# Attention, gated mixing and a gated projection on one core: the last product by seven block products, and smaller moves with it

## The chip, the cores and the metric

The kernel runs on one core of one Trainium2 chip. The metric is the device time of the program in microseconds; the kernel before takes 701.81 us, the median of three runs (699.28 to 704.09). All numbers in this document are float32 or float32r ("fp32r", the form of float32 that TensorE multiplies).

## The reference, cut to what matters

Three stages follow one another, for 4 batches of 576 tokens:

```python
# 1 attention: 8 heads of 64, causal, with a bias from a running sum of s
x = attention(q, k, v, s)                      # (4, 576, 512)
# 2 mixing with the previous token, then two gated products
k = np.maximum(xk @ w_k, 0.0)                  # 512 -> 1024
v = k * k @ w_v                                # 1024 -> 512
r = 1.0 / (1.0 + np.exp(-(xr @ w_r)))          # 512 -> 512
x = r * v
# 3 spatial gating
h = gelu_tanh(x @ w_in)                        # 512 -> 1024
u, v = (h[..., :d_ff // 2], h[..., d_ff // 2:])
v_n = (v - mu) / np.sqrt(var + 1e-06) * g_ln
v_s = np.einsum('ts,bsd->btd', w_sg, v_n) + b_sg[None, :, None]
gated = u * v_s
return (x + gated @ w_out).astype(np.float32)  # 512 -> 512
```

## The kernel before

Every float32 product is made of three fp32r products: each operand is split into a high half (the value cast to fp32r) and a low half (the value less its high half), and high times high, low times high and high times low are summed in one PSUM bank (a PSUM bank holds the sum of a chain of matmuls). The cast is a copy, mostly on ScalarE (ACT, helper `copy`, L71), the low half a subtraction on VectorE (DVE, helper `minus`, L74).

A scheduler orders each engine's instructions by a model of their times, within priorities that the code sets. Attention (generator `attend`) and the second stage (generator `moe1`) run interleaved until about 370 us; `moe1` goes over eight units of half a batch (288 tokens) and ends at about 506 us. In each unit `r` is made from a tanh: `rt = 0.5 * tanh(..) + 0.5` for a whole unit on DVE (L657), and then each of four tiles of `k*k @ w_v` is multiplied by it (L663) and stored to DRAM (`x2_d`). The weights come as 64-bit words; `convert` turns them into two halves.

The third stage goes batch by batch, from the loop at L975. Its functions, in the order of their matmuls for a batch b:

- `v_side(b)`: five row tiles of `v`, 56 matmuls, gelu on ACT, row statistics on DVE;
- `project(b-1)`: the last product of the batch before, `w_out` times gated, as eight tiles `po` of 128 x 288, 12 matmuls each (`mm3`, L690); DVE adds the residual `xf` (L943) and SyncE's queue stores each tile;
- `u_side(b)`: eight tiles `pu`, 12 matmuls each, gelu on ACT into `ut`;
- `norm(b)`: on DVE and ACT, beside the two above; the root by ACT's Sqrt, a reciprocal and one Newton step on DVE;
- `x_load(b+1)`: the next batch from DRAM and its halves;
- `gate(b)`: eight tiles `pg`, 14 matmuls each; for each tile DVE scales it (L930) and multiplies it by `ut` (L931) into `gf`, ACT casts the high half `gh`, DVE makes the low half `gl`.

All these tiles share six PSUM banks (`ps_b`): a matmul chain can start when the reader of the tile six places earlier is done. After the last batch `project` follows `gate` at once; elsewhere other matmuls lie between them.

Of the kernel before, what the change touches and what calls it, by code (L numbers as in the profile page):

```python
# [8 lines left out]
F32 = mybir.dt.float32  # L9
# [36 lines left out]
ENG = {"ia": "P", "mx": "D", "ca": "D", "p0": "P", "cl": "D", "qh": "D", "ql": "D", "kh": "A", "kl": "D", "vh": "A", "vl": "D", "xh": "A", "xl": "D", "fh": "A", "fl": "D", "rs": "D", "bh": "A", "bl": "D", "nh": "D", "nl": "D", "gh": "A", "gl": "D"}  # L46
# [6 lines left out]
def block_kernel(ctx: ExitStack, tc: tile.TileContext, qkv, vb, s, w_r, w_k, w_v, mu, w_in, w_out, w_sgT, g_ln, b_sg, out):  # L53
# [51 lines left out]
    def convert(w, c, n, t):  # L105
# [11 lines left out]
        nc.vector.scalar_tensor_tensor(ti, lw, 29, ti, ALU.logical_shift_right, ALU.bitwise_or)  # L117
        half = pool.tile([P, 2, 512], F32R, tag=name, name=name)
        copy("A" if att is not None else "D", half[:, 0], t)
        minus(ENG["cl"], half[:, 1], t, half[:, 0])  # L120
# [475 lines left out]
    def moe1():  # L596
# [29 lines left out]
        for u in range(2 * B):  # L626
# [30 lines left out]
            (nc.gpsimd if ENG["rs"] == "P" else nc.vector).tensor_scalar(rt, rt, 0.5, 0.5, ALU.mult, ALU.add)  # L657
            tc.cur_priority -= PM
            for m in range(4):
# [3 lines left out]
                nc.vector.tensor_tensor(rt[:, m], pm[:, 0:HD], rt[:, m], ALU.mult)  # L663
# [136 lines left out]
    def x_load(b):  # L800
        pool = pb if b % 2 else w2
        xf = pool.tile([P, 4, S], F32, tag="xf", name="xf")
        for hf in range(2):
            nc.sync.dma_start(xf[:, :, hf * HD : (hf + 1) * HD], x2_d[b][hf])
# [4 lines left out]
        xs[b] = xf, xh, xl, x4  # L809
        yield  # L810
        for c in range(4):
            copy(ENG["bh"], xh[:, c], xf[:, c])
            minus(ENG["bl"], xl[:, c], xf[:, c], xh[:, c])
            yield
        copy("D", x4[:, :, 0:D], xf[:, :, 4 * P :])
        minus("D", x4[:, :, D:], xf[:, :, 4 * P :], x4[:, :, 0:D])
# [3 lines left out]
    for size in moe1():  # L820
# [17 lines left out]
        if att is None and w2 is None:  # L838
# [5 lines left out]
            temps = w2.tile([P, 5, 512], F32, tag="vt", name="cvt")  # L844
            lws = conversions([(wi, c, n) for n in (1, 0) for c in range(4)], lambda i: temps[:, i % 5])
# [6 lines left out]
    def v_side(b, xh, xl, x4):  # L852
        vt = w2.tile([P, 5, DM], F32, tag="vt", name="vt")
        mv = mvs[b % 2]
        for t in range(5):
# [3 lines left out]
            if t < 4:  # L859
# [4 lines left out]
                nc.scalar.activation(vt[:, t], pv, AF.Gelu_apprx_tanh)  # L864
            else:
# [5 lines left out]
                vs = vt[:m, t]  # L871
# [4 lines left out]
            nc.vector.bn_stats(st[:m], vt[:m, t])  # L876
# [3 lines left out]
    def u_side(b, xh, xl):  # L880
        ut = pb.tile([P, 4, S], F32, tag="ut", name="ut")
        for m in range(4):
            for hf in range(2):
                hs = slice(hf * HD, (hf + 1) * HD)
                pu = ps_b.tile([P, 512], F32, tag="b", name="pu")
                mm3(pu[:, 0:HD], wi, m * P, xh[:, :, hs], xl[:, :, hs])
                nc.scalar.activation(ut[:, m, hs], pu[:, 0:HD], AF.Gelu_apprx_tanh)
        return ut

    def norm(b, vt, mv):  # L890
# [6 lines left out]
        nc.vector.tensor_tensor(t1, rs, rs, ALU.mult)  # L897
        nc.vector.tensor_tensor(t1, t1, var, ALU.mult)
        nc.vector.tensor_scalar(t1, t1, -0.5, 1.5, ALU.mult, ALU.add)
        nc.vector.tensor_tensor(rs, rs, t1, ALU.mult)  # L900
        vh, vl = ([xtp.tile([P, DM], F32R, tag=f"xt{t}", name=n) for t in range(4)] for n in ("vh", "vl"))
        v4 = const.tile([P, DM], F32R, tag="mask", name="v4")
        for t in range(5):
            m = P if t < 4 else D
            vs = vt[:m, t]
# [8 lines left out]

    def gate(b, ut, vh, vl, v4):
        gh = pb.tile([P, 4, S], F32R, tag="gh", name="gh")
        gl = pb.tile([P, 4, S], F32R, tag="gl", name="gl")
        for d in range(4):
            ds = slice(d * P, (d + 1) * P)
            for hf in range(2):  # L920
                hs = slice(hf * HD, (hf + 1) * HD)
                pg = ps_b.tile([P, 512], F32, tag="b", name="pg")
                for c in range(4):
                    nc.tensor.matmul(pg[:, 0:HD], vh[c][:, ds], wg[0][c][:, hs], start=(c == 0), stop=False)  # L924
                    nc.tensor.matmul(pg[:, 0:HD], vh[c][:, ds], wg[1][c][:, hs], start=False, stop=False)  # L925
                    nc.tensor.matmul(pg[:, 0:HD], vl[c][:, ds], wg[0][c][:, hs], start=False, stop=False)  # L926
# [4 lines left out]
                nc.vector.tensor_tensor(gf, gf, ut[:, d, hs], ALU.mult)  # L931
                copy(ENG["gh"], gh[:, d, hs], gf)
                minus(ENG["gl"], gl[:, d, hs], gf, gh[:, d, hs])
        return gh, gl

    def project(b, xf, gh, gl):
        for hf in range(2):
            hs = slice(hf * HD, (hf + 1) * HD)
            for m in range(4):
                po = ps_b.tile([P, 512], F32, tag="b", name="po")  # L940
                mm3(po[:, 0:HD], wo, m * P, gh[:, :, hs], gl[:, :, hs])
                ot = pb.tile([P, HD], F32, tag="ot", name="ot", bufs=3)
                nc.vector.tensor_tensor(ot, po[:, 0:HD], xf[:, m, hs], ALU.add)  # L943
                nc.sync.dma_start(out[b, m * P : (m + 1) * P, hs], ot)
# [4 lines left out]
    wg = [[], []]  # L949
    for c, tags in enumerate(SLOTS):  # L950
        if len(tags) == 2:
            halves = [w1p.tile([P, S], F32R, tag=t, name=f"wg{c}") for t in tags]
        else:
            place = xtp.tile([P, 2, S], F32R, tag=tags[0], name=f"wg{c}")
            halves = [place[:, 0], place[:, 1]]
# [90 lines left out]
```

## Time and profile before

| | |
|---|---|
| median of three runs | 701.81 us (699.28 to 704.09) |
| profiled execution | 701.87 us, of which the span from the first to the last instruction 700.0 us |
| TensorE (PE) busy | 666.8 us, 95% of the span, 4638 matmuls |
| VectorE (DVE) busy | 535.2 us, 76% |
| ScalarE (ACT) busy | 425.0 us, 61% |
| GpSimd (POOL) busy | 33.1 us, 5% |
| mean granted TensorE clock | 0.992 |

The profile is one execution. Busy time is the time in which an engine has an instruction under way; matmuls are pipelined, so the duration of one matmul is longer than the distance to the next, and what a matmul costs is read from the length of a whole chain. An idle stretch of an engine is put down to what released it.

### The profile page before, as it was taken

To read this page: it belongs to the slowest core of one execution; us is meant where nothing else is said; L and a number is where in the kernel's file an instruction comes from. 1 tells how busy PE (TensorE), PEld (TensorE's weight loads), DVE (VectorE), ACT (ScalarE), POOL (GpSimd) and SP (SyncE) were. 2 spreads that over 40 slices of the span, in tenths; PEclk is the share of its full clock that TensorE was granted. 3 is DMA by queue.
4 is the path that set the end of the run, shared out by engine and by line. 5 is a ranking of instruction groups with operands and counts; after the bars stand their busy time and mean duration, and the time that the engine had idled before them with its cause. 6 is when DMAs were issued, how large, how long until landed. Compare 5 with 4: busy or idle time off the path is not lost.

```text
span 700.0 us, 12906 instructions
## 1 busy us (share of the span) xinstructions
PE 666.8 (95%) x4638; PEld 620.8 (89%) x4638; DVE 535.2 (76%) x1341; ACT 425.0 (61%) x1011; POOL 33.1 (5%) x86
## 2 busy tenths in 40 slices
PE   7799888999998999999999999999999999999998
PEld 4578866988888989988999999999998998998997
DVE  8999899898989899899887796743847564564543
ACT  5789797778868986896895745725523233133120
POOL 6122100000000000000000000000000000000000
PEclk9999999999999999999999999999999999999999
DMA  8894442352443333423202700004240300300101
GB/s 267 238 286 152 148 137 63 92 154 80 126 118 101 90 109 93 133 81 108 85 22 79 272 10 35 1 18 163 67 112 18 119 1 15 122 2 9 60 1 68
DMA packets 39831, 67.47 MB, mean 96 GB/s; under 512 B 6908, under 2 KB 23400, under 8 KB 39736
## 3 DMA queue, kind: packets, MB, share of 16 engines
q1 hardware_dynamic: 39768, 66.66, 31.2%
q8 instruction: 36, 0.59, 0.4%
q14 instruction: 27, 0.22, 0.1%
HBM read 51.85 MB, written 10.19 MB: 89 GB/s over the span
## 4 chain that ended last, share of the span: by engine, by line
PE 64%; DVE 19%; ACT 6%; DMA 4%; issue 3%; SPq 2%; DVEq 0%; POOL 0%; ACTq 0%
PE m L677 25%; PE po L690 7%; PE pu L690 7%; DVE pr L374 3%; PE pg L925 2%; PE pg L926 2%; PE pg L924 2%; DMA rb<-rd 2%; DVE qk L74 2%; PE pv L863 2%; PE pv L862 2%; PE pv L861 2%; PE av L527 2%; DVE ptl L546 2%; ACT pr L400 2%
## 5 line engine op out<-in xcount | busy, mean ns | idle before, releaser
L400 ACT ACTIVATE pr<-pr,nm 128x448 f32<-128x448 f32 (+4 forms) x144 | 85.1, 592 | 21.2 <-DVE nm L374 20.6
L677 PE MATMUL m<-xh,wk 128*128 128x288 f32 x512 | 83.2, 301 | 0.0
L677 PE MATMUL m<-kh,wv 128*128 128x288 f32 x512 | 79.1, 297 | 0.0
L677 PEld LDWEIGHTS m<-xh,wk 128*128 128x128 f32 x512 | 73.1, 191 | 1.8 <-ACT xh L71 0.7
L677 PEld LDWEIGHTS m<-kh,wv 128*128 128x128 f32 x512 | 71.5, 188 | 0.4
L374 DVE CUSTOM_DVE_ANT_0 pr<-s,mask 128x448 f32<-128x448 f32 (+4 forms) x144 | 64.9, 453 | 8.3 <-PE s L360 6.5
L359 PE MATMUL s<-qk 128*128 128x288 f32 (+4 forms) x144 | 46.8, 327 | 8.6 <-DVE nh L374 5.9
L71 ACT CAST xh<-xf 128x288 fp32r<-128x288 f32 (+1 forms) x80 | 36.1, 480 | 22.7 <-DVE xf L616 10.7
L677 PE MATMUL m<-xl,wk 128*128 128x288 f32 x256 | 47.4, 301 | 0.0
L545 ACT CAST pth<-t 128x512 fp32r<-128x512 f32 (+1 forms) x72 | 38.2, 532 | 13.4 <-PE t L542 12.3
L360 PE MATMUL s<-qk 128*128 128x288 f32 (+4 forms) x144 | 44.1, 309 | 1.8 <-DVE kl L74 1.8
L546 DVE TENSOR_TENSOR ptl<-t,pth 128x512 fp32r<-128x512 f32 (+1 forms) x72 | 43.9, 614 | 2.2 <-ACT pth L545 1.9
L677 PE MATMUL m<-kl,wv 128*128 128x288 f32 x256 | 44.2, 299 | 0.0
L638 ACT ACTIVATE kf<-m 128x288 f32<-128x288 f32 x64 | 26.2, 411 | 28.7 <-PE m L677 28.2
L74 DVE TENSOR_TENSOR xl<-xf,xh 128x288 fp32r<-128x288 f32 (+1 forms) x80 | 39.0, 508 | 5.7 <-PE m L677 4.2
L71 ACT CAST gh<-gf 128x288 fp32r<-128x288 f32 x32 | 13.9, 433 | 45.8 <-DVE gf L931 45.8
L542 PE MATMUL t<-ident,pr 128*128 128x128 f32 x252 | 40.0, 277 | 1.6 <-DVE ptl L546 1.0
L677 PE MATMUL m<-xh,wr 128*128 128x288 f32 x256 | 40.8, 298 | 0.5 <-ACT kf L638 0.3
L610 ACT ACTIVATE xf<-xt,mu 128x288 f32<-128x288 f32 x64 | 33.4, 535 | 12.2 <-DVE xl L74 8.3
L690 PE MATMUL pu<-xh,wi 128*128 128x288 f32 x256 | 39.9, 295 | 0.0
L690 PE MATMUL po<-gh,wk 128*128 128x288 f32 x256 | 39.3, 296 | 0.0
L359 PEld LDWEIGHTS s<-qk 128*128 128x128 f32 x144 | 27.3, 190 | 12.9 <-DVE nh L374 8.1
(299 smaller groups left out, 1738.9 us busy)
## 6 DMA issues: line engine op xcount, KB each, us to landing
kld<-qkv SPq DMA_DIRECT2D x28, 288.0 KB
qld<-qkv SPq DMA_DIRECT2D x24, 288.0 KB
x_d<-rt SPq DMA_DIRECT2D x8, 576.0 KB
xf<-x_d SPq DMA_DIRECT2D x8, 576.0 KB
outT<-ot SPq DMA_DIRECT2D x32, 144.0 KB
vld<-qkv SPq DMA_DIRECT2D x24, 160.0 KB
qk<-qk SPq DMA_DIRECT2D x24, 144.0 KB
rb<-rd SPq DMA_DIRECT2D x24, 128.0 KB
```

The costliest lines, as they stand in the source:

```text
L71: nc.scalar.copy(dst, src) if eng == "A" else nc.vector.tensor_copy(dst, src)
L74: (nc.gpsimd if pick(engines) == "P" else nc.vector).tensor_tensor(dst, a, b.bitcast(F32), ALU.subtract)
L359: nc.tensor.matmul(dst, qk[0][:, 0, qs], qk[0][:, 1, ks], start=True, stop=False)
L360: issued[0] = nc.tensor.matmul(dst, qk[1][:, 0, qs], qk[1][:, 1, ks], start=False, stop=True)
L374: nc.vector.tensor_tensor_reduce(out=dst, in0=src, in1=msk, scale=-0.125, scalar=first, op0=ALU.add, op1=ALU.min, accum_out=acc)
L400: i = nc.scalar.activation(dst, dst, AF.Exp, bias=nm[:, col : col + 1], scale=-1.0, accum_out=w.sm[:, col : col + 1])
L542: issued[0] = nc.tensor.transpose(bank[:, o : o + P], x, ident)
L545: nc.scalar.copy(pth[:, cols], bank[:, 0:o])
L546: nc.vector.tensor_tensor(ptl[:, cols], bank[:, 0:o], pth[:, cols].bitcast(F32), ALU.subtract)
L610: nc.scalar.mul(xf, xp, mu1[:, j, c : c + 1])
L677: i = nc.tensor.matmul(dst, w(x, c, m), xx[:, c], start=(n + c == 0), stop=(n == 2 and c == w.nk - 1))
L690: nc.tensor.matmul(dst, w(x, c, m), xx[:, c], start=(n + c == 0), stop=(n == 2 and c == w.nk - 1))
```

## The change

The last product becomes one with seven block products where there were eight (Strassen's, in Winograd's form): `w_out` and gated are cut in two by two blocks, sums and differences of blocks of `w_out` are made once (`quarters`: three blocks as they are, four sums), those of gated once a batch in `gate` (tile `tf`, halves kept in `tp`), and `project` makes, for each of two row halves, seven products of six matmuls and joins them with sums `u`. For this:

- `project` has 84 matmuls a batch where it had 96. DVE adds six sums `u` a batch; the residual is read again from DRAM into `ot` and GpSimd adds `u` to it (`emit`; in the last batch it lies in `xr`, and half of these adds are DVE's); DVE adds the PSUM tile, as before. One product of each half is copied out of PSUM by ACT.
- `gate` goes through the second half of its tiles in another order (right half first), and each batch has eight subtractions and eight pairs of halves for `tf` more, two pairs fewer for `gh` and `gl`.
- `w_out` is no longer converted to halves by `conversions`, but assembled, summed and split in `quarters`, which comes after the first batch's `gate`. `project` of the first batch moves behind `u_side(1)`.
- `norm`'s root is three Newton steps from an integer start, all on DVE; ACT needs no Sqrt, and the program holds 2 loads of ACT's function tables where it held 11. `vh` is cast by ACT where DVE did it.
- `x_load` fetches half a batch at a time into one buffer, and the tiles `vt` and `ut` are two pieces each.
- `rt`'s scaling at L657 is gone: the factor 0.5 goes into `wv`'s halves, and the product takes `rt + 1` in the same instruction.

The diff, cut to its core:

```diff
+        if w is wv:
+            nc.scalar.mul(half[:, 0], t, 0.5)
+            nc.vector.scalar_tensor_tensor(half[:, 1], t, 0.5, half[:, 0].bitcast(F32), ALU.mult, ALU.subtract)
...
-            (nc.gpsimd if ENG["rs"] == "P" else nc.vector).tensor_scalar(rt, rt, 0.5, 0.5, ALU.mult, ALU.add)
...
-                nc.vector.tensor_tensor(rt[:, m], pm[:, 0:HD], rt[:, m], ALU.mult)
+                nc.vector.scalar_tensor_tensor(rt[:, m], rt[:, m], 1.0, pm[:, 0:HD], ALU.add, ALU.mult)
...
-        nc.scalar.activation(rs, var, AF.Sqrt)
-        nc.vector.reciprocal(rs, rs)
+        nc.vector.tensor_scalar(rs.bitcast(I32), var.bitcast(I32), 1, 0x7FFFFFFF, ALU.logical_shift_right, ALU.bitwise_xor)
+        nc.vector.tensor_scalar(rs, rs, 0.33885 * 2.0**-64, None, ALU.mult)
         t1 = const.tile([P, 5], F32, tag="t1", name="t1")
...
+        for _ in range(3):
+            nc.vector.tensor_tensor(t1, rs, rs, ALU.mult)
+            nc.vector.scalar_tensor_tensor(t1, t1, -0.5, var, ALU.mult, ALU.mult)
+            nc.vector.scalar_tensor_tensor(rs, t1, 1.5, rs, ALU.add, ALU.mult)
...
+    def halves(k, c, x):
+
+        copy("A", tp[k][0][c], x)
+        minus("D", tp[k][1][c], x, tp[k][0][c])
...
+                if d < 2 and hf:
+                    nc.vector.tensor_tensor(tf[:, 0, c], gf, ut[d // 2][:, d % 2, hs], ALU.mult)
+                    less(tf[:, 1, c], tf[:, 0, c], last)
+                    halves(1, c, tf[:, 1, c])
+                    continue
+                nc.vector.tensor_tensor(gf, gf, ut[d // 2][:, d % 2, hs], ALU.mult)
+                if d >= 2:
+                    if hf:
+                        less(tf[:, 1, c], gf, tf[:, 1, c])
+                        less(tf[:, 0, c], gf, tf[:, 0, c])
+                    else:
+                        less(tf[:, 1, c], gf, tf[:, 1, c])
                 copy(ENG["gh"], gh[:, d, hs], gf)
                 minus(ENG["gl"], gl[:, d, hs], gf, gh[:, d, hs])
+                if d >= 2:
+                    for k, x in ((2, 1), (3, 0)) if hf else ((4, 1),):
+                        halves(k, c, tf[:, x, c])
...
+            for y, z in ((0, 0), (1, 0), (0, 1)):
+                for c in range(2):
+                    nc.tensor.matmul(dst, wq[a][:, y, c, ms], x[z][c], start=(n == 0), stop=(n == 5))
...
+            if last:
+                ot = xr[:, i, hs]
+            else:
+                pool, n = ((pb, 3), (w2, 2))[outs[0] % 5 // 3]
+                outs[0] += 1
+                ot = pool.tile([P, HD], F32, tag="ot", name="ot", bufs=n)
+                nc.sync.dma_start(ot, x2_d[b][hf][:, i])
+            (nc.vector if last and m else nc.gpsimd).tensor_tensor(ot, ot, u, ALU.add)
+            add(ot, ot, bank)
+            nc.sync.dma_start(out[b, i * P : (i + 1) * P, hs], ot)
+
+        for m in range(2):
+            ms = slice(m * P, (m + 1) * P)
+            u1, u2 = place(0), place(1)
+            nc.scalar.copy(u1, part("11", block(0, 0)))
+            add(u2, u1, part("s2", tp[2]))
+            emit(m, 0, u1, part("12", block(1, 0)))
+            u3 = place(2)
+            add(u3, u2, part("s3", tp[3]))
+            p5 = part("s1", tp[1])
+            emit(2 + m, 1, u3, p5)
+            add(u2, u2, p5)
+            emit(m, 1, u2, part("s4", block(1, 1)))
+            emit(2 + m, 0, u3, part("22", tp[4]))
```

The scheduler orders the new instructions. The three places below show what it made of them where it matters for the argument. Names: `po` and `p`, `ps` are PSUM tiles of the projection (after the change one each block product, in the order 11, s2, 12, s3, s1, s4, 22 of the code); numbers behind a name tell tiles apart.

DVE after the last tile of the last batch's `gate`, before the change: it finishes the tile and then only adds the residual.

```order
L930 SCALAR_TENSOR_TENSOR gf<-pg,g_sb,b_sb 128x288
L74 TENSOR_TENSOR gl<-gf,gh 128x288
L931 TENSOR_TENSOR gf<-gf,ut 128x288
L74 TENSOR_TENSOR gl<-gf,gh 128x288
L943 TENSOR_TENSOR ot<-po,xf 128x288 x8
```

Behind the last tile's two products stand one subtraction and the eight adds.

The same place on DVE after the change, from the last tile's first instruction to the add that frees tile `p_8627` (product 12).

```order
L957 SCALAR_TENSOR_TENSOR gf<-pg,g_sb,b_sb 128x288
L74 TENSOR_TENSOR gl<-gf,gh 128x288
L74 TENSOR_TENSOR wg_6314<-tf,tp 128x288
L74 TENSOR_TENSOR wg_6294<-tf,wg_6304 128x288
L963 TENSOR_TENSOR gf<-gf,ut_7682 128x288
L937 TENSOR_TENSOR tf<-gf,tf 128x288
L993 TENSOR_TENSOR us<-ps_8619,us 128x288
L74 TENSOR_TENSOR gl<-gf,gh 128x288
L993 TENSOR_TENSOR us<-ps_8637,us 128x288
L74 TENSOR_TENSOR tp<-tf,tp 128x288
L1014 TENSOR_TENSOR xr<-xr,us 128x288
L993 TENSOR_TENSOR xr<-ps_8645,xr 128x288
```

Two more rows, `us<-ps_8645,us` and `xr<-p_8627,xr`, follow there. Where three instructions stood between the last gate tile and the adds, a mix of gate work and sums stands now.

DVE at the end of the program after the change, behind the sums of product s3 of the second half.

```order
L1014 TENSOR_TENSOR xr<-xr,us 128x288
L993 TENSOR_TENSOR xr<-ps_8710,xr 128x288
L993 TENSOR_TENSOR us<-ps_8710,us 128x288
L993 TENSOR_TENSOR xr<-p_8731,xr 128x288
L1014 TENSOR_TENSOR xr<-xr,us 128x288
L993 TENSOR_TENSOR xr<-ps_8721,xr 128x288
```

Behind the add of the last product (`p_8731`) two more adds stand now; before, the add of the last tile was DVE's last instruction.

PE at the start of the last projection, before the change: tile after tile, all from `gh` and `gl`.

```order
L927 MATMUL pg<-wg_6338,v_8223 128x288
L928 MATMUL pg<-wg_6338,v_8223 128x288
L690 MATMUL po<-gh,wk_6601 128x288
L690 MATMUL po<-gh,wk_6609 128x288
L690 MATMUL po<-gh,wk_6617 128x288
```

Nothing of the gate but `gh` and `gl` is needed for this.

The same place on PE after the change: single matmuls of products s2, 12 and s3 are started early, and 12 is finished only after s3 and s4.

```order
L988 MATMUL p_8611<-gh,w_6829 128x288 x4
L988 MATMUL p_8611<-gl,w_6829 128x288 x2
L988 MATMUL ps_8619<-tp,ws_6851 128x288
L988 MATMUL p_8627<-gh,w_6832 128x288
L988 MATMUL ps_8637<-wg_6305,ws_6844 128x288
L988 MATMUL ps_8645<-gh,ws_6839 128x288 x4
L988 MATMUL ps_8645<-gl,ws_6839 128x288 x2
L988 MATMUL ps_8656<-gh,ws_6848 128x288 x4
L988 MATMUL ps_8656<-gl,ws_6848 128x288
L988 MATMUL ps_8619<-tp,ws_6851 128x288 x3
```

Products that need the last tile's sums have moved behind those that need only earlier ones.

DVE beside the projection of the second and the third batch, which the norm of the next batch shares; before the change, from the second residual add on.

```order
L943 TENSOR_TENSOR ot<-po,xf 128x288
L892 TENSOR_SCALAR var<-mv_6296 128x5
L895 RECIPROCAL rs<-rs 128x5
L897 TENSOR_TENSOR t_8210<-rs 128x5
L898 TENSOR_TENSOR t_8210<-t_8210,var 128x5
L943 TENSOR_TENSOR ot<-po,xf 128x288
L899 TENSOR_SCALAR t_8210<-t_8210 128x5
L900 TENSOR_TENSOR rs<-rs,t_8210 128x5
L906 TENSOR_SCALAR vt<-vt,mv_6296,rs 128x512 x4
```

Three adds are through before the wide steps of the norm begin.

The same stretch after the change.

```order
L993 TENSOR_TENSOR u<-ps_7560,u 128x288
L907 TENSOR_SCALAR var<-mv_6290 128x5
L909 TENSOR_SCALAR rs<-var 128x5
L910 TENSOR_SCALAR rs<-rs 128x5
L913 TENSOR_TENSOR t_7800<-rs 128x5
L914 SCALAR_TENSOR_TENSOR t_7800<-t_7800,var 128x5
L993 TENSOR_TENSOR ot<-ps_7568,ot 128x288
L993 TENSOR_TENSOR u<-ps_7568,u 128x288
L915 SCALAR_TENSOR_TENSOR rs<-t_7800,rs 128x5
L993 TENSOR_TENSOR ot<-p_7593,ot 128x288
```

Sums `u` stand between the residual adds, and the wide steps of the norm (L906, now L921) come later against them.

## Rows read from the trace of the kernel before

**Rows 1.** Windows by stage: start:end, us, busy us (count) of each engine, clock, DMA.

```profile
100.00:150.00 50.00, 45.91 (x316) 41.56 (x316) 46.81 (x126) 37.88 (x96) 2.34 (x7) 0.97 0.35 101
...
350.00:500.00 150.00, 149.38 (x1081) 145.61 (x1082) 106.98 (x239) 88.50 (x192) 0.71 (x3) 1.00 0.22 75
500.00:696.70 196.70, 196.69 (x1357) 188.46 (x1355) 108.11 (x252) 53.91 (x106) 0.00 (x0) 1.00 0.15 48
```

**Rows 2.** Waits of PE from 125 to 350 us: total us, times, longest.

```profile
PE s L359 <- DVE nh L374: 5.9, 8, 1.7
PE av L527 <- DVE ptl L546: 2.7, 4, 1.6
```

**Rows 3.** Chain of waits that ended last, from 530 us: start, us, what.

```profile
537.04 12.79 PE po L690 x96
...
683.89 12.81 PE po L690 x96
696.73 0.46 DVE ot L943
```

**Rows 4.** Groups by line, 480 to 700 us: shapes, count, busy us, mean ns, idle before.

```profile
L930 DVE SCALAR_TENSOR_TENSOR gf<-pg,g_sb,b_sb 128x288 f32<-128x288 f32 x32 | 16.5, 515 | 27.0 <-PE pg L928 26.8
L74 DVE TENSOR_TENSOR gl<-gf,gh 128x288 fp32r<-128x288 f32 x32 | 14.4, 451 | 3.8 <-ACT gh L71 3.6
L943 DVE TENSOR_TENSOR ot<-po,xf 128x288 f32<-128x288 f32 x32 | 14.2, 452 | 9.8 <-PE po L690 9.6
...
L887 ACT ACT_TABLE_LOAD x4 | 5.1, 1283 | 31.3 <-PE pu L690 31.3
```

**Rows 5.** Timeline of DVE in the last gate: first instruction of its last two tiles.

```profile
682.07 0.52 DVE L930 SCALAR_TENSOR_TENSOR gf<-pg,g_sb,b_sb 128x288 f32<-128x288 f32 x1 [0.60 <-PE pg L928]
...
683.92 0.52 DVE L930 SCALAR_TENSOR_TENSOR gf<-pg,g_sb,b_sb 128x288 f32<-128x288 f32 x1 [0.61 <-PE pg L928]
```

**Rows 6.** Timeline of DVE beside the second projection (590 to 605 us).

```profile
595.75 2.36 DVE L906 TENSOR_SCALAR vt<-vt,mv,rs 128x512 f32<-128x512 f32 x5
...
604.03 0.82 DVE L943 TENSOR_TENSOR ot<-po,xf 128x288 f32<-128x288 f32 x2
```

**Rows 7.** Timeline of POOL, 0 to 88 us: its widest arithmetic.

```profile
15.13 1.40 POOL L454 TENSOR_SCALAR pr<-pr,rc 128x128 f32<-128x128 f32 x1 [1.97 <-DVE rc L412]
...
43.98 0.85 POOL L454 TENSOR_SCALAR pr<-pr,rc 128x128 f32<-128x128 f32 x1 [0.63 <-PE t L438]
...
54.97 1.88 POOL L74 TENSOR_TENSOR qk<-qld,qk 64x256 fp32r<-64x256 f32 x2 [7.98 <-DMA vb<-vb]
...
79.93 0.73 POOL L74 TENSOR_TENSOR qk<-qld,qk 64x256 fp32r<-64x256 f32 x1 [6.13 <-issue]
86.61 0.92 POOL L74 TENSOR_TENSOR qk<-qld,qk 64x256 fp32r<-64x256 f32 x1 [5.96 <-ACT qk L71]
```

**Rows 8.** Timeline of DVE around those, 54 to 86 us.

```profile
54.67 0.67 DVE L116 SCALAR_TENSOR_TENSOR cvt<-wr20w,cvt 128x512 int32<-128x512 int32 x1
...
56.18 1.21 DVE L117 SCALAR_TENSOR_TENSOR cvt<-wr20w,cvt 128x512 int32<-128x512 int32 x1
...
80.25 0.96 DVE L74 TENSOR_TENSOR wv<-cvt,wv 128x512 fp32r<-128x512 f32 x1
85.89 0.68 DVE L74 TENSOR_TENSOR wv<-cvt,wv 128x512 fp32r<-128x512 f32 x1
```

**Rows 9.** Lines L657, L663 and L616: ns min/median/max, first and last start.

```profile
L657 DVE TENSOR_SCALAR rt<-rt x8: 702/751/762, 127.5 to 493.9; 128x1152 f32<-128x1152 f32 x8
...
L663 DVE TENSOR_TENSOR rt<-m,rt x32: 396/456/459, 131.8 to 505.9; 128x288 f32<-128x288 f32 x32
...
L616 DVE SCALAR_TENSOR_TENSOR xf<-xt,mu_sb,xf x64: 466/510/610, 26.3 to 461.0; 128x288 f32<-128x288 f32 x64
```

**Rows 10.** Timeline of DVE at the start of the first gate.

```profile
505.92 0.46 DVE L663 TENSOR_TENSOR rt<-m,rt 128x288 f32<-128x288 f32 x1 [1.09 <-PE m L677]
516.60 0.29 DVE L71 CAST x<-xf 128x256 fp32r<-128x256 f32 x1 [10.22 <-DMA xf<-x_d]
```

More of the change, by code (lines that the diff above doesn't have):

```diff
@@ L656, in moe1 @@
             tc.cur_priority += PM
-            (nc.gpsimd if ENG["rs"] == "P" else nc.vector).tensor_scalar(rt, rt, 0.5, 0.5, ALU.mult, ALU.add)
+            if not more:
+                nc.scalar.activation(first, rt[:, 3, 0:1], AF.Gelu_apprx_tanh)
             tc.cur_priority -= PM
@@ L852, in v_side @@
     def v_side(b, xh, xl, x4):
-        vt = w2.tile([P, 5, DM], F32, tag="vt", name="vt")
+        vt = value_rows("vt")
         mv = mvs[b % 2]
@@ L880, in u_side @@
     def u_side(b, xh, xl):
-        ut = pb.tile([P, 4, S], F32, tag="ut", name="ut")
+        ut = [pb.tile([P, 2, S], F32, tag=f"ut{k}", name=f"ut{k}") for k in range(2)]
+        last = []
         for m in range(4):
@@ L961, in block_kernel @@
-            minus("D", halves[1][:, hs], raw, halves[0][:, hs])
+            i = nc.scalar.copy(place[0][:, hs], raw)
+            if last is not None:
+                behind(i, last[7])
+            minus("D", place[1][:, hs], raw, place[0][:, hs])
         for x in range(2):
-            wg[x].append(halves[x])
+            wg[x].append(place[x])
+    for c in range(3):
+        spatial(c, mw, "xf")
     wo = Weight(w1p, "wk", w_out)
-    temps = w1p.tile([P, 2, 512], F32, tag="wk01", name="cvt")
@@ L966, in block_kernel, with quarters, split, fold @@
-    cos = conversions([(wo, i, 0) for i in range(4)], lambda i: temps[:, i % 2])
+    wq = {}
+    def quarters(last):
+        ta = w1p.tile([P, 2, 512], F32, tag="wk01", name="cvt")
+        tb = w1p.tile([P, 2, 512], F32, tag="wr30", name="cvt")
+        for c in range(4):
+            load_words(wo, c, 0)
+        for c in range(4):
+            assemble(wo, c, 0, (ta, tb)[c // 2][:, c % 2])
+        a11, a21, a12, a22 = (t[:, :, i * 256 : (i + 1) * 256] for t in (ta, tb) for i in range(2))
+        def split(name, pool, tag, x):
+            w = wq[name] = pool.tile([P, 2, 2, 256], F32R, tag=tag, name="w" + name)
+            behind(nc.scalar.copy(w[:, 0], x), last[5 if name[0] == "s" else 3])
+            minus("D", w[:, 1], x, w[:, 0])
+        def fold(dst, x, y, op):
+            nc.vector.tensor_tensor(dst, x, y, op)
+        split("11", w1p, "wk00", a11)
+        split("12", w1p, "wk10", a12)
+        split("22", w1p, "wk20", a22)
+        fold(a22, a21, a22, ALU.add)
+        split("s1", w1p, "wk30", a22)
+        fold(a21, a11, a21, ALU.subtract)
+        fold(a11, a22, a11, ALU.subtract)
+        split("s3", xtp, "xh", a21)
+        fold(a12, a12, a11, ALU.subtract)
+        split("s4", xtp, "xl", a12)
+        split("s2", w1p, "wr30", a11)
@@ L972, in block_kernel @@
     b_sb = pb.tile([P, S], F32, name="b_sb")
+    place = pb.tile([P, 6, HD], F32R, name="tp")
+    pb.tile([P, 408], F32, name="gap")
+    pb.tile([P, 2, S], F32, tag="ut0", name="ut0")
     nc.sync.dma_start(b_sb, b_sg.to_broadcast([P, S]))
+    pieces += [place[:, k] for k in range(6)]
+    tp = {k: [[pieces.pop() for c in range(2)] for x in range(2)] for k in (4, 2, 3)}
+    outs = [0]
     tail = None
     for b in range(B):
-        xf, xh, xl, x4 = xs.pop(b)
+        xh, xl, x4 = xs.pop(b)
         vt, mv = v_side(b, xh, xl, x4)
-        if b:
+        if b > 1:
             project(*tail)
-        ut = u_side(b, xh, xl)
+        ut, last = u_side(b, xh, xl)
+        if b == 0:
+            for c in (3, 4):
+                spatial(c, w2, "u", None)
         vh, vl, v4 = norm(b, vt, mv)
-        for _ in cos:
-            pass
         for _ in x_load(b + 1) if b + 1 < B else ():
             pass
+        if b == 1:
+            project(*tail)
         gh, gl = gate(b, ut, vh, vl, v4)
-        tail = (b, xf, gh, gl)
+        if b == 0:
+            quarters(last)
+        tail = (b, gh, gl)
     project(*tail)
```

117 lines of the change are left out of this document (71 added, 46 removed).

## The prediction

> **What bounds the kernel now.** I read the windows by stage first. From 350 us on TensorE has hardly an idle moment: 149.38 us busy of 150, then 196.69 of 196.70, at a granted clock of 1.00, while VectorE is busy for 108.11 of those 196.70 us and ScalarE for 53.91 [rows 1]. In this half an instruction of another engine counts only if it makes TensorE wait, and a matmul that is taken away counts in full. Before 350 us it is the other way about: from 100 to 150 us PE has 45.91 us of 50 and DVE 46.81, and the list of PE's waits names DVE and its products, with `s` behind `nh` for 5.9 us in eight waits and `av` behind `ptl` for 2.7 us in four [rows 1, 2]. There DVE's work is worth something. The chain that ended last shows the end of the program: 96 matmuls of `po` in 12.81 us, then one add of 0.46 us on DVE [rows 3].
>
> **Term a, fewer matmuls.** The price of one is read from a whole chain: 12.79 us / 96 = 0.1332 us [rows 3]. The change takes 12 from each of four batches: 48 x 0.1332 = **-6.4 us**, all of it on the path. Nothing else that PE does is dropped.
>
> **Term b, the last batch, where the projection follows the gate at once.** Before, a gate tile costs DVE one L930 (515 ns), one product by `ut` and one `gl` (451 ns; I take the product at the same price, same shape and type) [rows 4]: 24 instructions, 8 x 0.515 + 16 x 0.451 = 11.3 us, against 8 x 14 x 0.1332 = 14.9 us of matmuls. DVE keeps pace: it idles 0.60 us before each tile, and the tiles come 1.85 us apart [rows 5]. After the change the gate has eight subtractions, eight `tf` low halves and two `gl` fewer: 38 instructions, 8 x 0.515 + 30 x 0.451 = 17.7 us. They are not spread evenly. The first four tiles have 14 of them (6.6 us in 7.5 us of matmuls), the last four 24: 4 x 0.515 + 20 x 0.451 = 11.1 us in 7.5 us. Besides, every tile waits on DVE for ACT's cast before the low half. So DVE ends the gate some 11.1 - 7.5 + 1.4 = 5 us after PE, the 1.4 being what it does for the last tile in any case (L930, product, `gl`). The order shows how the scheduler meets this: PE starts with products that need only early tiles (11, then parts of s2, 12 and s3, then s1 and s4), 36 to 48 matmuls, or 4.8 to 6.4 us. Then it needs a bank, and of the six the next one to come free is that of product 12, whose add on DVE stands behind the last gate work, three sums and an add without PSUM: about 5 + 7 x 0.45 = 8.1 us after PE's last gate matmul. PE waits 8.1 - 6.4 = 1.7 us. At the end three adds stand behind the last product instead of one: the last product's own, a sum of two SBUF tiles and one more from PSUM, 3 x 0.452 = 1.36 against 0.46 us [rows 3, 4], so +0.9. Term b is **+2.6 us**. Its bounds: DVE on time, with the end alone, +0.5 (half of the tail hidden in the last product); nothing started early, so that the whole 5 us is waited for less what banks cover, +4.
>
> **Term c, the projections of the second and the third batch.** They share DVE with the norm. Here DVE has no slack already before: the five wide steps L906 take 595.75 to 598.11, and the last two residual adds run from 604.03 to 604.85 [rows 6], while the second projection's tiles have left PE by then. After the change this stretch gets six sums (6 x 0.452 = 2.7 us) and four more small Newton steps, and loses four casts of `vh` to ACT. I take DVE as 2 us later. The tiles of `u_side` that follow need the banks; their slack I put at 0.3 to 0.5 us each, so of 2 us about 1 can be caught up over two places. What GpSimd does beside it comes on top: while POOL has the subtractions at 54.97 and 79.93 us [rows 7], DVE's instructions are longer than their neighbours, L117 with 1.21 us where L116 of the same shape has 0.67, and `wv` 0.96 where the one at 85.89 has 0.68 [rows 8]. A disturbed DVE instruction thus costs 0.28 to 0.54 us, and a projection has eight POOL adds: 2.2 to 4.3 us of DVE time, most of it in DVE's idle half. In sum I take **+1.0 us** for both projections, bounds 0 and 4.
>
> Beside [rows 8] stands a rule that speaks against this change: the Trainium skill, "SBUF — State Buffer", section "Who interferes with whom", says that a DVE instruction with two SBUF inputs contends with a GpSimd instruction, and that whichever issues first holds the shared ports for the whole instruction. The trace agrees as far as two pairs of rows can show it. By the rule in full, each of eight adds would stop DVE for its whole length, term c would go towards its upper bound, and the sum to about 700; by the rows it stays at 698.3.
>
> **Term d, L657.** Eight instructions of 751 ns are gone, four of them before 350 us where DVE counts; the product L663 (456 ns) becomes a form with a scalar, which at L616 takes 510 [rows 9]: 4 x 0.75 - 16 x 0.05 = 2.2 us less of DVE there. Of a DVE gain PE gets only what it waited for on DVE, and the waits of [rows 2] are spread over other tiles: **-0.8 us**, bounds -2.1 and 0.
>
> **Costed at nothing.** Nine table loads at 1283 ns go from ACT [rows 4]; ACT is busy for 27% of this stage, so PE gets nothing. The first batch: `quarters` (seven splits with a DVE part, four sums) comes behind the first gate and its matmuls wait for none of it, since project(0) stands behind `u_side(1)`; but with the 6.4 us more of gate work DVE does some 17 us more, against 10.2 us of idle time that it had at the start of this stage [rows 10]. It falls behind by up to 7 us, and six banks cover 6 x 1.86 = 11 us of gate matmuls. If that cover is gone, up to 1.5 us is lost; this goes into the range. `x_load` in halves, `vt` and `ut` in pieces only free buffers earlier. The 24 residual loads add little to a DMA share of 0.15 [rows 1]; they stand on SP's queue ahead of the stores, five can be ahead of their use, and the last three wait for stores of tiles 1.6 us apart. `wv`'s halves take as many instructions as before.
>
> **The sum.** Profiled 701.87, which the median 701.81 equals within 0.1: 701.87 - 6.4 + 2.6 + 1.0 - 0.8 = **698.3 us**, a gain of 0.5%. One per cent, 7 us, is about what a measurement of this kernel can tell from no change.
>
> **Rival 1: all of it is hidden.** DVE has 88 us of idle time behind 500 us, and the scheduler reorders around each wait. Then only the smallest tail remains and attention takes the whole of term d: 701.87 - 6.4 + 0.5 - 2.1 = **693.9**. For it speaks that PE's chains in [rows 3] have no gap before; against it that 24 of 38 gate instructions lie in the last four tiles.
>
> **Rival 2, slower: GpSimd's adds are too dear.** POOL is idle in this stage before [rows 1], so no row has this add. The nearest by operation, a two-input sum of 64 x 256, takes 0.73 to 0.94 us (the latter half of 1.88 for two), which by width is 0.82 to 1.06 for 288; the nearest by partitions, L454 with 128 x 128, 0.85 to 1.40, is 1.9 to 3.1 [rows 7]. I take 1.0, since the operation is the same. Eight adds a projection must fit in 11.2 us of products and some 3.2 us that two banks cover: the point from which it decides is 14.4 / 8 = 1.8 us. At 2.5, the middle of the upper row, 20.0 - 14.4 = 5.6 us are lost at each of three projections, and the time is 698.3 + 16.8 = **715**; at 2.0 it is 703.
>
> The Trainium skill, "GPSIMD Engine Reference", section 3.1, has 4497 ns for a sum of 2048 elements a partition; an estimate by it is 0.63 us for 288, nearer to the lower row, and the sum would stay.
>
> **Rival 3: the order moves elsewhere.** Attention's instructions are swapped in a few places, the first batch's DVE work backs up behind the first gate; what is gained at the projections is lost there: +3, or **701.5**.
>
> **How the numbers follow.** The forecast's case (terms within their bounds, 695 to 701) has 0.60; rival 1 0.18; rival 2 0.15, of which 0.08 lie up to 708.9 and 0.07 beyond; rival 3 0.07. The range cuts the tip of rival 1 (0.05) and the dearer part of rival 2 (0.13): 693.8 to 703. Faster by over 1% (below 694.8) is rival 1, 0.18; slower by over 1% 0.07; within 1% the rest, 0.75.
>
> **What would show it.** Chains of 84 matmuls a batch, 11.2 us, and PE's busy time 6.4 lower (term a). In the last projection a wait of PE behind `xr<-p_8627` of 1 to 3 us, and three adds at the end (b). Waits in `u_side` behind sums or residual adds, and POOL's adds at about 1.0 us (c and rival 2: adds at 2 us with `u_side` waiting behind them would prove it). PE's idle time from 125 to 350 us smaller by about 1 us (d). The forecast is wrong if PE waits in the gates of the first three batches, or if POOL's adds stretch DVE's own beyond 0.3 us each.

## The result and the profile after

The changed kernel takes 693.33 us (median of four runs, 692.17 to 695.74), the kernel before beside it 700.96 us: ratio 0.9899, interval 0.9867 to 0.9932. A second set of runs of the same two gave 695.27 against 700.48 us, ratio 0.9918 (0.9891 to 0.9945). By the two ratios the gain is 5.7 to 7.1 us; 3.5 were forecast. The first median lies 0.5 us below the range of 693.8 to 703 us. But the kernel before, too, was a little faster beside it than the 701.81 us that it was known by; at the first ratio those become 694.7 us, inside the range.

The windows by stage of the changed kernel (start:end, us, then busy us and count of PE, weight loads, DVE, ACT and POOL, clock, DMA share and GB/s) answer to [rows 1]:

```profile
100.00:150.00 50.00, 47.19 (x326) 42.92 (x325) 45.74 (x123) 37.52 (x97) 1.99 (x6) 0.97 0.36 106
350.00:500.00 150.00, 148.83 (x1076) 145.02 (x1075) 101.59 (x230) 85.81 (x193) 0.70 (x3) 1.00 0.24 83
500.00:690.60 190.60, 186.66 (x1282) 178.42 (x1280) 143.76 (x341) 65.66 (x144) 27.99 (x28) 1.00 0.22 69
```

DVE has 36 us more to do behind 500 us, POOL 28 us that it had not, and the list of PE's waits behind 500 us is empty; the 3.9 us in which PE isn't busy there are the end, after its last matmul. The chain that ended last shows that end (start, us, what), against [rows 3]:

```profile
683.47 2.39 PE ps L988 x18
685.86 0.81 PE p L988 x6
686.67 0.03 issue
686.70 0.46 DVE xr L993
687.15 0.38 DVE xr L1014
687.53 0.02 issue
687.55 0.46 DVE xr L993
```

Three DVE instructions in 1.31 us where one took 0.46. The rest of the end, the store of the last tile, is the same: 2.7 us behind the last add, 2.8 before.

One view measures the third stage far more closely than whole runs do: from the first matmul of the first gate to the end of the span. The timeline of PE has that matmul, in the kernel before and in the changed one:

```profile
509.00 0.29 PE L924 MATMUL pg<-wg,vh 128*128 128x288 f32 x1
```

```profile
505.38 0.30 PE L951 MATMUL pg<-wg,vh 128*128 128x288 f32 x1
```

Before, 700.0 - 509.00 = 191.0 us; after, 690.7 - 505.38 = 185.3 us. The last matmul ends at 696.68 and at 686.66 us, so the matmuls' part went from 187.68 to 181.28 us, -6.40 us, which is 48 matmuls at 0.1332 us, and the end grew by 0.7 us (3.3 to 4.0). Ahead of the last matmul all the sums, differences and adds cost PE nothing that can be read here.

What lies ahead of the first gate, 3.6 us less here, is another matter: it differs between executions of one kernel. In a table, with the profiles of the experiments (us; "clock" is the mean granted TensorE clock of the profiled execution, "stage" is from the first gate's first matmul to the end of the span):

| kernel | ratio to before (interval) | clock | first gate | last matmul ends | span | stage |
|---|---|---|---|---|---|---|
| before | | 0.992 | 509.00 | 696.68 | 700.0 | 191.0 |
| before again | 0.9988 (0.9965 to 1.0010) | 0.993 | 509.52 | 697.20 | 700.5 | 191.0 |
| changed | 0.9899 (0.9867 to 0.9932) | 0.992 | 505.38 | 686.66 | 690.7 | 185.3 |
| changed again | 0.9918 (0.9891 to 0.9945) | 0.985 | 509.78 | 691.22 | 695.3 | 185.5 |
| eight products | 0.9989 (0.9973 to 1.0005) | 0.990 | 505.76 | 693.26 | 696.5 | 190.7 |
| before with the fold | 1.0016 (0.9993 to 1.0039) | 0.992 | 506.31 | 694.06 | 697.3 | 191.0 |
| changed, no fold | 0.9934 (0.9912 to 0.9956) | 0.985 | 511.84 | 694.29 | 698.3 | 186.5 |
| rt work added | 1.0052 (1.0024 to 1.0080) | 0.987 | 520.50 | 702.29 | 706.3 | 185.8 |
| adds on DVE | 0.9910 (0.9890 to 0.9929) | 0.992 | 504.35 | 686.14 | 690.5 | 186.2 |
| gate's low halves twice | 0.9935 (0.9911 to 0.9959) | 0.991 | 505.83 | 688.92 | 693.7 | 187.9 |
| norm's low halves twice | 0.9898 (0.9870 to 0.9925) | 0.992 | 505.43 | 686.72 | 690.8 | 185.4 |
| old norm | 0.9910 (0.9886 to 0.9935) | 0.991 | 506.09 | 688.31 | 692.5 | 186.4 |
| spread gate | 0.9882 (0.9859 to 0.9905) | 0.994 | 505.47 | 687.03 | 691.5 | 186.0 |
| spread gate, adds on POOL | 0.9890 (0.9863 to 0.9916) | 0.992 | 506.79 | 688.10 | 692.0 | 185.2 |

For the two kernels with two profiles the stages agree to 0.2 us, so differences of half a microsecond can be read there.

### The profile page after: what moved, and what is told of

It reads as the page before. It is cut to its first block, busy times and chain, and to the rows that moved or that the text cites. A ratio compares the mean times of both kernels' runs of the same rounds, so it can differ in the third digit from the quotient of the medians.

```text
span 690.7 us, 13031 instructions
## 1 busy us (share of the span) xinstructions
PE 659.9 (96%) x4590; PEld 614.5 (89%) x4590; DVE 565.1 (82%) x1424; ACT 437.2 (63%) x1058; POOL 62.4 (9%) x114
## 4 chain that ended last, share of the span: by engine, by line
PE 62%; DVE 20%; ACT 6%; DMA 6%; issue 4%; SPq 2%; POOL 0%; DVEq 0%; ACTq 0%
PE m L687 23%; PE pu L700 7%; PE ps L988 4%; DVE pr L383 4%; DMA rb<-rd 3%; PE p L988 3%; PE pg L952 2%; PE pg L953 2%; PE pg L951 2%; PE pv L876 2%; PE pv L875 2%; PE pv L877 2%; DVE qk L74 2%; DVE ptl L555 2%; ACT pr L409 2%
## 5 line engine op out<-in xcount | busy, mean ns | idle before, releaser
L1014 POOL TENSOR_TENSOR ot<-ot,u 128x288 f32<-128x288 f32 x24 | 24.4, 1032 | 263.9 <-DVE v L927 181.7
L619 ACT ACTIVATE xf<-xt,mu 128x288 f32<-128x288 f32 x64 | 33.4, 537 | 10.7 <-DVE xl L74 5.7
L687 PEld LDWEIGHTS m<-xh,wr 128*128 128x128 f32 x256 | 36.1, 188 | 2.3 <-ACT kf L647 1.3
```

The costliest lines, as they stand in the source:

```text
L687: i = nc.tensor.matmul(dst, w(x, c, m), xx[:, c], start=(n + c == 0), stop=(n == 2 and c == w.nk - 1))
```

## The experiments

**What the seven products are worth.** In this kernel `project` has eight block products again, 12 matmuls a tile, without sums, and the gate makes no differences of blocks; the rest of the change stays.

```diff
-        for m in range(2):
-            u1, u2 = place(0), place(1)
...
+        for hf in range(2):
+            for i in range(2):
+                for m in range(2):
+                    ms = slice(m * P, (m + 1) * P)
+                    emit(2 * i + m, hf, None, part((("11", "12"), ("21", "22"))[i], [block(j, hf) for j in range(2)]))
```

Expected: 

> The changed kernel with eight block products again (12 matmuls a tile, no sums on DVE, no adds on GpSimd, the gate without differences of blocks); all the rest of the change stays. Theory 1, all that the seven products add to DVE, ACT and GpSimd is hidden but for the tail: 48 matmuls back is +6.4, the tail 0.7 shorter, so 5.7 us more than the changed kernel, ratio 0.997 to 0.999. Rival, the sums cost PE something that the profile doesn't show as waits (2 to 3 us): only 3 to 4 us more, ratio 0.993 to 0.996.

Measured: 700.19 us, ratio 0.9989, stage 190.7 us. Against the two profiles of the changed kernel the stage is 5.2 to 5.4 us longer, the matmuls' part (187.50 us) 6.1 to 6.2. Theory 1 holds: the products give what their count says to within 0.3 us, less the end. It also says what all the other edits give together: 0.1% (0.05% more to 0.27% less), about 0.8 us, which the interval doesn't tell from nothing.

**Whether the first 500 us changed.** The changed kernel and the kernel before once more, unaltered.

Expected of the changed one: 

> The changed kernel unaltered, to have its ratio beside the others of this set. If the 3.6 us that its first profile gained before the first gate belong to the change: ratio 0.986 to 0.989. If they are spread between executions and the change is worth its matmuls and its tail alone, 6.4 - 0.7 = 5.7 us: ratio 0.991 to 0.993, and the first gate starts anywhere from 504 to 512 us.

Expected of the kernel before: 

> The kernel before unaltered, for a second profile of it. If the start of its first gate at 509.0 us was one draw of a spread between executions, as 505.4 and 509.8 us are in two profiles of the changed kernel, this one lies anywhere from 504 to 512 us. If the change moves it by 3.6 us, it lies at 508.5 to 509.5 us. From there to the end 191.0 us in either case.

Measured: the changed kernel's first gate starts at 509.78 us at a mean granted clock of 0.985, where it was 505.38 at 0.992: 4.4 us between two executions of one program, and the ratio, 0.9918, is the one expected if the 3.6 us are such a spread. The kernel before came out at 509.52 us, where the change as the cause would have it to within 0.1 us. The table leans the same way: at a granted clock of 0.990 or more, the nine profiles of kernels with the fold of the next experiment start the first gate at 504.35 to 506.79 us, the two without it at 509.00 and 509.52. But these two are from the upper end of the kernel's times: 701.87 and 702.39 us, where its 42 runs at such a clock in the three sets of experiments have a median of 700.2 (698.38 to 702.83). By an estimate from these medians the 3.6 us in the pair of profiles thus hold some 2 us of draw.

**The fold of the half into wv (term d).** Once alone in the kernel before, once taken out of the changed one.

```diff
+        if w is wv:
+            nc.scalar.mul(half[:, 0], t, 0.5)
+            nc.vector.scalar_tensor_tensor(half[:, 1], t, 0.5, half[:, 0].bitcast(F32), ALU.mult, ALU.subtract)
-            (nc.gpsimd if ENG["rs"] == "P" else nc.vector).tensor_scalar(rt, rt, 0.5, 0.5, ALU.mult, ALU.add)
-                nc.vector.tensor_tensor(rt[:, m], pm[:, 0:HD], rt[:, m], ALU.mult)
+                nc.vector.scalar_tensor_tensor(rt[:, m], rt[:, m], 1.0, pm[:, 0:HD], ALU.add, ALU.mult)
```

Expected in the kernel before: 

> The kernel before with only the receptance's half folded into wv (L657 gone, its product with the scalar form). Theory 1, the stretch before 505 us gained 3.6 us in the profiled execution because DVE work of L657 (0.75 us an instruction) stood on the path: 697.5 to 699.5 us, ratio 0.995 to 0.998, and the first gate starts 2 to 3.5 us earlier than at 509.0. Rival, those 3.6 us are only the spread between executions (699.3 to 704.1 before): ratio 0.999 to 1.001.

Expected without it in the changed one: 

> The changed kernel with L657 and the plain product put back. Theory 1: what the fold gives is lost again, 2 to 3.5 us, ratio to the kernel before 0.993 to 0.995. Rival (the fold gives nothing): ratio 0.989 to 0.991 as for the whole change. In both the stretch from the first gate to the last matmul stays at 181.3 us.

Measured: alone it gives nothing that the runs show (701.74 us, ratio 1.0016; at a granted clock of 0.990 or more 699.7 us, median of five, against 700.3). Its profile has the first gate at 506.31 us, 2.7 us earlier, as theory 1 said, but that execution is the fastest of its twelve (699.12 us). Taken out of the changed kernel the fold costs about 2.7 us (696.0 us against 693.3, medians of six and of four runs at such a clock), though the intervals of the two ratios overlap. In its profile the third stage is 1.1 us longer, where neither expectation had a change; PE idled 0.6 there before one product of the first projection, for ACT's copy of another. The two kernels don't agree, so the third experiment makes the cost large: three instructions in each unit that multiply `rt` by one and add zero.

```diff
+            for _ in range(3):
+                nc.vector.tensor_scalar(rt, rt, 1.0, 0.0, ALU.mult, ALU.add)
```

Expected: 

> The changed kernel with three instructions on DVE in each of the eight units of the second stage that multiply rt by one and add zero, three times the cost of the old L657: 12 x 0.75 = 9 us more DVE work before 370 us. Theory of the prediction (about a third of such DVE time reaches PE: 0.8 of 2.2 us): 3 us more, ratio 0.994 to 0.997. Rival (DVE's time there hides behind waits that other things end): under 1 us more, ratio 0.989 to 0.992.

Measured: 704.66 us, ratio 1.0052, 10.6 us over the changed kernel (703.9 against 693.3, granted clock 0.990 or more; by the ratios 9.4 to 10.7). The first gate starts at 520.50 us, in a profile that is 4.6 us above its kernel's median at such a clock. Both expectations were too low. The four units before 350 us hold 12 x 0.75 = 9 us of it, and those behind add nothing: between the stores of the fourth unit's and the seventh unit's result lie 136.3 us with it and 136.0 without. So DVE's time there reaches the end about in full, not by a third. PE's waits from 125 to 350 us (what waited for what: us, times, longest), in the changed kernel first and with the added work behind it, show where, beside [rows 2]:

```profile
PE s L368 <- DVE nh L383: 5.2, 6, 1.7
PE av L536 <- DVE ptl L555: 2.2, 3, 0.9
PE t L551 <- DVE ptl L555: 1.0, 3, 0.4
PE s L368 <- DVE nm L383: 0.3, 1, 0.3
```

```profile
PE av L536 <- DVE ptl L555: 6.4, 8, 2.4
PE s L368 <- DVE nh L383: 3.8, 5, 1.8
PE t L551 <- DVE ptl L555: 2.1, 5, 0.6
PE m L689 <- DVE rt L675: 0.7, 1, 0.7
PE s L368 <- DVE nm L383: 0.3, 1, 0.3
```

The added work itself is waited for only once (0.7 us); it is `av`, queued behind `ptl` on DVE, that waits longer. All waits of the list together grow by 4.6 us (8.7 to 13.3), less than half of the loss; by which way the rest reaches PE it doesn't show.

**DVE in the last batch (term b).** The low halves of the differences are written twice in the last gate (`LOW[0]` is 2 there and 1 elsewhere).

```diff
-        minus("D", tp[k][1][c], x, tp[k][0][c])
+        for _ in range(LOW[0]):
+            minus("D", tp[k][1][c], x, tp[k][0][c])
```

Expected: 

> The changed kernel with the low halves of the differences (L74 into tp and wg) written twice in the last batch's gate: eight more DVE instructions of 0.45 us, six of them in the last four tiles, +2.7 to 3.6 us of DVE work. Theory 1 (the last projection starts with so many matmuls that need no late tile that DVE is on time with nothing to spare: one bank comes free 0.1 us before PE writes it): the wait of PE and the tail grow by 2 to 3.5 us, ratio 0.992 to 0.995, PE idle in the last chain. Rival (there is cover left in the banks, or the order gives way): under 1 us, the last chain within 0.5 us of 11.45.

Measured: stage 187.9 us, some 2.5 more for eight instructions of 0.45 us, 1.8 of it in PE's last chain (13.26 us where it was 11.45) and 0.7 behind it. DVE is on time in the changed kernel with nothing to spare. The timelines of the changed kernel show how close it is; DVE first, with the sum of the first s2, the gate's last low half and the add of product 12:

```profile
679.52 0.46 DVE L993 TENSOR_TENSOR us<-ps,us 128x288 f32<-128x288 f32 x1
...
680.63 0.45 DVE L74 TENSOR_TENSOR tp<-tf,tp 128x288 fp32r<-128x288 f32 x1
...
682.72 0.45 DVE L993 TENSOR_TENSOR xr<-p,xr 128x288 f32<-128x288 f32 x1
```

PE in the same stretch:

```profile
675.21 0.69 PE L988 MATMUL p<-gh,w 128*128 128x288 f32 x4
...
680.05 0.77 PE L988 MATMUL p<-gh,w 128*128 128x288 f32 x4
...
681.58 0.69 PE L988 MATMUL ps<-tp,ws 128*128 128x288 f32 x4
...
682.52 0.69 PE L988 MATMUL p<-gh,w 128*128 128x288 f32 x4
```

PE leaves the gate at 675.21 us, DVE at 681.08: 5.9 us late. But the sum of the first s2 reads its bank at 679.52, among the gate's last work, ends at 679.98, and PE starts the first product of the second half 0.07 us later, at 680.05. Two more products of that half, s2 and 12, start at 681.58 and 682.52, still ahead of the add of product 12 (682.72). With the low halves twice it is the same sum, later; DVE, then PE:

```profile
681.93 0.45 DVE L994 TENSOR_TENSOR us<-ps,us 128x288 f32<-128x288 f32 x1
```

```profile
682.43 0.79 PE L989 MATMUL p<-gh,w 128*128 128x288 f32 x4 [0.34 <-DVE us L994]
```

The sum ends at 682.38 and the same product starts 0.05 us later, 6.77 us behind the gate where it was 4.84. Ahead of that PE waits 0.5 us for ACT's cast of the last `gh`, which itself comes behind DVE.

Half of the differences can be made earlier: the last gate in the order 0, 2, 1, 3; and, in a second kernel, the last adds of `emit` on GpSimd as well.

```diff
-        for d in range(4):
+        for d in (0, 2, 1, 3) if b + 1 == B else range(4):
...
-            (nc.vector if last and m else nc.gpsimd).tensor_tensor(ot, ot, u, ALU.add)
+            nc.gpsimd.tensor_tensor(ot, ot, u, ALU.add)
```

Expected of the order alone: 

> The changed kernel, but the last batch's gate goes through its column blocks in the order 0, 2, 1, 3, so that half of the differences are made in the first four tiles (19 DVE instructions behind the start of the last four tiles where there were 24, same number in all). Theory 1 (in the last batch DVE's work is the path: eight instructions more cost 2.55 us): from the first gate's start to the end 0.5 to 1 us less than the 185.3 to 185.5 of the unaltered kernel, most of it behind the last matmul (4.04 us there). Rival (the three adds at the end are set by the order of the products, not by DVE's backlog): within 0.2 us of 185.4. The ratio of whole runs can't tell these apart.

Expected of both: 

> The same with all adds of emit on GpSimd in the last batch too, four fewer instructions on DVE. Theory 1 (each DVE instruction of the last batch counts): another 0.4 to 1 us less than the kernel with the spread gate alone. Rival (a GpSimd add holds DVE's instructions up for its 0.8 us, as those of 128 x 5 were held): no gain or up to 0.5 us lost against the spread gate alone.

Measured: stage 186.0 and 185.2 us against 185.3 to 185.5. The order alone lost some 0.6 us where theory 1 had a gain and its rival no change: DVE ends the gate 5.2 us behind PE instead of 5.9, but then idles 0.85 us for ACT's copy of a product (0.48 in the changed kernel). With the adds on GpSimd the loss is won back: 0.8 us less than with the order alone, as theory 1 of the second kernel had it. But neither beats the changed kernel by more than its profiles differ.

**The norm beside the projections (term c).** Its low halves twice, in the third and fourth batch.

```diff
-                minus(ENG["nl"], vl[t], vs, vh[t])
+                for _ in range(2 if b > 1 else 1):
+                    minus(ENG["nl"], vl[t], vs, vh[t])
```

Expected: 

> The changed kernel with the low halves of the normalised rows (vl, four of 0.64 us) written twice in the third and fourth batch's norm, +2.5 us of DVE work beside the second and the third projection. Theory of the prediction (the banks of u_side's tiles have 0.3 to 0.5 us to spare): 1.5 to 2 us lost at each of the two, ratio 0.993 to 0.996, PE idle in u_side behind DVE. Rival (the adds are through before the wide steps and u_side's 12.8 us cover the norm): no change, ratio as the unaltered kernel's, u_side 12.9 us long.

Measured: stage 185.4 us, no loss. The last add now starts at 605.50 us:

```profile
604.88 0.69 DVE L74 TENSOR_TENSOR vl<-vt,vh 128x512 fp32r<-128x512 f32 x1
605.50 0.45 DVE L994 TENSOR_TENSOR ot<-ps,ot 128x288 f32<-128x288 f32 x1
```

The same add in the changed kernel:

```profile
603.13 0.46 DVE L993 TENSOR_TENSOR ot<-ps,ot 128x288 f32<-128x288 f32 x1
```

It comes 2.4 us later with the added work, and `u_side` runs without a gap in both. The slack that the prediction put at 0.3 to 0.5 us was at least 2.3 (the two profiles start the stage 0.05 us apart).

**The old norm.** Sqrt on ACT with its tables, `vh` cast on DVE.

Expected: 

> The changed kernel with the norm as before the change (Sqrt on ACT with its table loads, one Newton step, vh cast on DVE). Theory 1, the prediction's: ACT is idle most of this stage and PE waits for neither, no change within 1 us. Rival (beside GpSimd's adds and the six sums DVE's four casts of 0.4 us and ACT's loads of 1.28 us before each gelu come in the way): 1 to 3 us more, PE idle in u_side.

Measured: stage 186.4 us, 0.9 to 1.1 more than the changed kernel, spread over the first three projections and the end: the chains are 11.76, 11.53 and 11.51 us where they were 11.30 or 11.31 (11.45 for the first in the second profile), the end 4.2 where it was 4.0. That is at the edge of theory 1's 1 us, and the place is the projection and not `u_side`, as its rival had it. The list of PE's waits names none of it. Which half of it does this, the tables or the casts, was not separated.

**GpSimd's adds.** All of them on DVE.

```diff
-            (nc.vector if last and m else nc.gpsimd).tensor_tensor(ot, ot, u, ALU.add)
+            nc.vector.tensor_tensor(ot, ot, u, ALU.add)
```

Expected: 

> The changed kernel with all 28 adds of emit on DVE, none on GpSimd. Theory 1 (GpSimd's adds make DVE lose about as much as they take from it, since DVE's instructions of 128 x 5 took 0.55 to 0.80 us beside them and 0.16 elsewhere): 8 x 0.45 = 3.6 us more on DVE a projection, 2 to 3 us of stalls less, no change beyond 1 us, ratio 0.988 to 0.992. Rival (GpSimd's help is needed, DVE frees the last bank only 0.3 us before u_side wants it): 2 to 3 us a projection lost at the second and third, ratio 0.994 to 0.998, PE waiting in u_side on DVE.

Measured: 694.99 us, ratio 0.9910, stage 186.2 us, 0.8 more, of which 0.5 lie in the last chain (PE waits 0.4 us there for a sum on DVE) and 0.3 behind it. Theory 1 holds: the second and third projections are as long as with GpSimd (11.31 us). For the norm's first step, one line of DVE (duration in ns, least, median and most) reads in the changed kernel and, behind it, in this one:

```profile
L909 DVE TENSOR_SCALAR rs<-var x4: 172/484/800, 432.7 to 640.4; 128x5 int32<-128x5 int32 x4
```

```profile
L909 DVE TENSOR_SCALAR rs<-var x4: 163/166/172, 431.7 to 640.0; 128x5 int32<-128x5 int32 x4
```

An instruction of 0.17 us takes up to 0.80 beside a GpSimd add, which takes 0.80 itself. It goes the other way, too: the timeline of POOL in the changed kernel, beside DVE's `vl` (597.32 to 600.1 us):

```profile
588.64 1.57 POOL L1014 TENSOR_TENSOR ot<-ot,u 128x288 f32<-128x288 f32 x2 [1.41 <-DVE var L907]
597.47 4.10 POOL L1014 TENSOR_TENSOR ot<-ot,u 128x288 f32<-128x288 f32 x2 [4.43 <-DMA ot<-x_d]
```

Two adds take 1.57 us in the first row, while DVE's small instructions wait for them, and 4.10 in the second, where DVE has a run of instructions with two SBUF inputs. That is what the Trainium skill says in "SBUF — State Buffer", section "Who interferes with whom": whoever issues first has the shared ports for the whole instruction. The trace agrees on DVE's side, with 0.17 against up to 0.80 us, one add's length. GpSimd's 3.3 us against 0.8 is more than one DVE instruction: it spans four subtractions and ends 0.7 us behind the last of them. PE waited for none of it, so it cost this kernel nothing; DVE itself waited 4.8 us in all for GpSimd's adds.

## Why the prediction was right, and where it was off

The direction and the chain of reasons held: TensorE is the bound, matmuls that go count in full, and the new work is nearly all beside them. The size was half of it, and the case that came true is rival 1 (all of it hidden, 693.9 us). That its number fits so well is partly luck: its sum starts from 701.87 us and takes 2.1 us for term d, of which the runs show about 1.

- **Term a** (-6.4) is right: -6.40 us between the first two profiles, 6.1 to 6.2 when it is undone in the changed kernel, and 48 matmuls fewer (4590 of 4638).
- **Term b** was +2.6 and is +0.7. The end was +0.9 forecast and 0.7 measured. The step that failed is the wait of 1.7 us: "of the six the next one to come free is that of product 12". DVE's lag was about right (5 us forecast, 5.9 measured), and the time of that add came out (8.1 us behind the gate; 682.72 + 0.45 - 675.21 = 8.0), partly by luck: the order has six DVE instructions for the sum's seven, and the 0.48 us of waiting for ACT's copy made up for it. But the banks that PE took first were those whose sums stood among the gate's last work: it needed one after 36 matmuls, 4.84 us behind the gate, as the prediction's lower figure says, and had it 0.07 us after the sum of s2. Nor does a tile wait for the reader of the tile six places earlier in PE's order, as "The kernel before" has it: PE starts three products of the second half ahead of product 12's add. The order had shown the sum, in the rows where `us<-ps_8619` stands ahead of the last subtractions. With some 2.5 us lost for eight more instructions, and PE behind the same sum, the mechanism itself is shown; it was only not reached.
- **Term c** was +1.0 and is 0 in the stage. The step that failed is the slack of 0.3 to 0.5 us a tile, an assumption without a row; at least 2.3 us were there. The charge for GpSimd was right as a mechanism and was hidden: DVE's instructions were stretched by 0.39 to 0.63 us, beyond the 0.3 that the prediction names as a sign of being wrong, and PE lost nothing by it.
- **Term d** was -0.8. Everything but the products is worth some -0.8 us by the kernel with eight products, which its interval doesn't tell from nothing; the new norm, costed at nothing, saves 1.0 us of the stage beside the seven products. PE's idle time from 125 to 350 us is 1.2 us smaller, as forecast (9.2 where it was 10.4). That DVE time ahead of 350 us counts by a third is wrong: 9 us of it cost 10.6. By that the fold should give its upper bound, 2 us and more; taken out of the changed kernel it shows 2.7, put into the kernel before none, or 0.6 by the runs at a clock of 0.990 or more. What the fold is worth by itself stays open; that the scheduler rearranges attention with each such edit may be why the two differ, which no run here shows.
- **Rival 2** is out: GpSimd's add takes 0.80 us undisturbed and 1.03 on the mean of the first three projections (1.0 was taken), and the adds could all have stood on DVE at 0.8 us. **Rival 3**: no PE wait in the first gates.

The pair of profiles (-9.3 us) overstates the gain: -5.7 in the third stage, and -3.6 ahead of it, of which about 1 is the change by an estimate from the runs at a granted clock of 0.990 or more (700.2 - 693.3 = 6.9, less 5.7).

## What to carry to other kernels

Where one engine is busy without a gap, instructions taken from it can be booked in full, and the work that replaces them costs only where it stands ahead of the reader that frees the buffer this engine needs next: follow the order to the bank that comes free first, not to the step that ends last. A slack that no row shows is a guess; writing one instruction twice measures it. And compare stages between fixed points of two profiles: here that told 0.2 us, where whole runs told 2.

## What the runs showed of the hardware

- A DVE instruction of 128 x 5 takes 0.17 us alone and 0.55 to 0.80 beside a GpSimd add of 0.80; a GpSimd add takes up to 3.33 us beside DVE's subtractions of 128 x 512. The Trainium skill's figure for such an add ("GPSIMD Engine Reference", section 3.1, some 0.63 us by estimate for 288) is below the 0.80 measured.
- The sum with a scalar (L673) takes 453 ns at the median, as the plain product did (456 in [rows 9]); the 54 ns that were charged for the form, by L616 with two inputs from SBUF, don't show here.
- One program's time goes with its mean granted TensorE clock: 42 runs of the kernel before at 0.990 or more have a median of 700.2 us, 23 below it 703.2, and between two profiles of the changed kernel, at 0.992 and 0.985, the first gate moved by 4.4 us. The clock is at its lower level (0.50) for stretches of a few us, most of them ahead of 125 us: in the slower of the two from 92 to 101 us, with PE busy for all 9.00 us, and once behind, from 225 to 228. From 350 us to the first gate's start and through the stage the profiles show 1.00.
